# Issuing the whole start of a fused attention and feed-forward kernel from one written list, with eight GpSimd operations on VectorE and added products of zeros on TensorE

## The chip, the core and the metric

The kernel runs on one core of a Trainium2 chip. The metric is the device time of one execution in microseconds. An execution of the kernel before took 555.93 us (median of three, 555.01 to 556.05).

## What is computed

```python
# attention: a, B, C, x per batch (4), head (8), 768 positions; head_dim 32, d_state 16
L = np.exp(cum[:, :, :, None] - cum[:, :, None, :]) * causal      # decay between positions
y_intra = ((C @ B.T) * L) @ x
y_inter = (C @ state) * np.exp(cum)
state = decay_full * state + sum(B x * decay_from_j)              # from chunk to chunk
x = y.transpose(0, 2, 1, 3).reshape(3072, 256)
h = np.maximum(np.maximum(x @ w1, x @ w2), x @ w3)                # first layer, 768 wide
x = h @ w_out
x = (1 / (1 + np.exp(-(x @ w_gate))) * (x @ w_val)) @ w_out2      # second layer, 1536 wide
```

## The kernel before

The positions are cut into 8 chunks of 96, and the 32 pairs of batch and head into 8 groups of four. A step of the attention is one group of one chunk; there are 64 steps. For step k (chunk c, group g) the program makes:

- for k below 16, a masked copy of C on ScalarE (L327); later chunks get B and C split into three bfloat16 parts instead (`split_bc`, with a subtraction on GpSimd, L312, and twelve small transfers into `bi` and `cs`),
- the score products `s` of four units on TensorE (L332 or L335), into one of three PSUM buffers that the hidden layer uses too (tag `up`),
- the decay factors: `load_decay` brings the raw decays of two steps into `dec` (four buffers), broadcast to 128 partitions, and two scans on VectorE (L291) turn them into running products. The decays have to be clipped first: `clip_all` loads all of them, clips them on VectorE and stores them in device memory (`ad`), from where every later load comes; the first two loads are clipped on the spot (L287),
- `mt`: the state part on GpSimd (L340), the weighted scores on VectorE (L347),
- the output products `y` (L356); after four steps the outputs are copied to `xt_hi` (ScalarE, L366) and `xt_lo` (VectorE, L368), and the carried state is transposed into the next chunk's x (`xs`, VectorE, four L372).

The two feed-forward layers work on eight token tiles of 512 columns. For tile t and each of six blocks m of the first layer's width, three banks u are made, each from two times three products of 128x512 (a high and a low half of both operands, L406 to L408); ScalarE copies the first bank (L484), VectorE takes the maximum with the second and third (L486, L488), ScalarE and a low-half operation (GpSimd L479, in the last tiles VectorE) split the result into `hi` and `lo`, and six products add it to the output banks `o` one block later (`down`).

The first layer's weights arrive as 64-bit floats in twelve pieces, a00 to a51 (block, half), and are decoded: three ScalarE operations, one on VectorE (L178), an add on GpSimd (L183), a cast on ScalarE (L211), a low half on GpSimd (L213).

The order of the work is set by generators. Each step, decode or eviction is a generator that stands in `Pipe`; every `tick` moves each one a stage on. Ahead of the tiles 12 steps (`START`) are ticked through, and then one step or more per slot as `UNTIL` says: 24 steps are out when tile 0 ends. `BEHIND` says after which decay load how many weight pieces are loaded. All loads are issued by SyncE's one queue, in program order. The program's scheduler then orders the instructions of each engine.

```python
    for k in range(START + 6):
        if k < START:
            att_step(LEAD)
        if k == 4:
            load_x(1, slice(16, 32))
        pipe.tick()
    for _ in range(9):
        pipe.tick()
        weights_tick()
```

Of the kernel before, what the change touches and what calls it, by code (L numbers as in the profile page):

```python
# [19 lines left out]
CH = 96  # L20
# [21 lines left out]
START = 12  # L42
# [3 lines left out]
LEAD = 2  # L46
# [6 lines left out]
BEHIND = {4: 1, 5: 1, 6: 2, 7: 2, 8: 2, 9: 1, 10: 1, 11: 1, 12: 1}  # L53
# [18 lines left out]
def scan_attention_then_ffn(ctx: ExitStack, tc: tile.TileContext, xh, ah, bch, pick, bn, w1, w2, w3,  # L72
# [56 lines left out]
    def piece1(m, part):  # L129

        cols = slice(256 * m, 256 * m + 256)
        loads = [[up1[0][:, :, cols], up1[1][:, :, cols]],
                 [up1[2][:, :, cols], dn1[:, m, :].rearrange("p (d f) -> p d f", d=2)]][part]
        return wp1, wt1.setdefault(m, []), loads, f"a{m}{part}"

    todo = [(piece1, m, part) for m in range(M1) for part in range(2)]
# [7 lines left out]
    def load_weights():  # L144

        f, m, part = todo.pop(0)
        wpool, blocks, loads, name = f(m, part)
        raw = wpool.tile([128, 2 * len(loads), 128, 2], I32, tag=name, name=f"raw_{name}")
        for k, s in enumerate(loads):
            sp.dma_start(out=raw[:, 2 * k:2 * k + 2].rearrange("p b n t -> p b (n t)"), in_=s)  # L150
        loaded.append((raw, wpool, blocks, name))

    def decode(raw, wpool, blocks, name):
        nb = raw.shape[1]
        second = name[0] != "a"

        def behind(k):
            return tc.issue_after(evict[k].ins) if second else ExitStack()
# [5 lines left out]
        with behind(0):  # L164
            act.activation(out=sg.bitcast(F16).rearrange("p b (n t) -> p b n t", t=2)[..., 1], in_=f1.bitcast(F32),
                           func=AF.Identity, scale=2.0 ** -112)
        if second:
            yield
        with behind(0):
            act.mul(f1.bitcast(F32), f1.bitcast(F32), 2.0 ** -112)  # L170
        if second:
            yield
# [7 lines left out]
        if second:  # L180
            yield
        with behind(1):
            (dve if second else pool).tensor_tensor(out=r, in0=t, in1=r, op=ALU.add)  # L183
        yield
        if second:
            hi, lo = store2(wpool, blocks, name)
            parts = [(r.bitcast(F32), slice(0, 4))]
            if name[0] != "d":
                v = r.bitcast(F32)
                q = wq[0].tile([128, 3, 128], F32, tag="q", name=f"q_{name}")  # L190
                for k, (out, x, y, op) in enumerate(((q[:, 0], v[:, 1], v[:, 3], ALU.add),
                                                     (q[:, 2], v[:, 0], v[:, 1], ALU.subtract),
                                                     (q[:, 1], q[:, 0], v[:, 0], ALU.subtract),
                                                     (v[:, 1], v[:, 2], q[:, 1], ALU.subtract))):
                    with behind(1):
                        dve.tensor_tensor(out=out, in0=x, in1=y, op=op)
                    if k % 2:
                        yield
                parts.append((q, slice(4, 7)))
            for x, at in parts:  # L200
                with behind(0):
                    act.copy(hi[:, at], x)
                yield
            for x, at in parts:
                with behind(1):
                    dve.tensor_tensor(out=lo[:, at], in0=x, in1=hi[:, at].bitcast(F32),
                                      op=ALU.subtract)
            return
        w = wpool.tile([128, 2, nb, 128], F32R, tag=name, name=f"w_{name}")
        blocks += [(w[:, 0, b], w[:, 1, b]) for b in range(nb)]  # L210
        act.copy(w[:, 0], r.bitcast(F32))  # L211
        yield
        pool.tensor_tensor(out=w[:, 1], in0=r.bitcast(F32), in1=w[:, 0].bitcast(F32),  # L213
                           op=ALU.subtract)
# [17 lines left out]
    def constants():  # L232

        pool.memset(delta_s, 0.0)
        for y in ys:
            act.copy(y[:, :, CH + N:128], delta_s[:, 0:4, 0:128 - CH - N])
        for r in range(4):
# [7 lines left out]
            pool.memset(d[:, r, 0:1], 1.0)  # L245
        act.copy(delta, delta_s)
# [7 lines left out]
    pk = acon.tile([128, NG], F32, name="pk")  # L254

    def clip_all():

        t = awk.tile([128, 2, LW], F32, tag="ac", bufs=1, name="ac")
        sp.dma_start(out=t.rearrange("p u w -> p (u w)"),
                     in_=ah.rearrange("r (s w) -> (r s) w", s=4))  # L260
        dve.tensor_scalar(out=t[:, :, 1:LW], in0=t[:, :, 1:LW], scalar1=1e-6, scalar2=1.0,
                          op0=ALU.max, op1=ALU.min)
        yield
        sp.dma_start(out=ad.rearrange("r (s w) -> (r s) w", s=4),
                     in_=t.rearrange("p u w -> p (u w)"))

    def load_decay(n, src):
        t = awk.tile([128, PU, LW], F32, tag="dec", bufs=DECS, name=f"dec{n}")
        i = sp.dma_start(out=t.rearrange("p u w -> p (u w)"), in_=src[n].partition_broadcast(128))
        dec[n] = t  # L270
        for _ in range(BEHIND.get(n, 0)):
            with tc.issue_after(i.ins):
                load_weights()
# [508 lines left out]
```

## Time and profile before

| | us |
|---|---|
| median of three runs | 555.93 |
| the profiled execution, its time | 554.77 |
| the profiled execution, its span | 553.0 |
| TensorE busy in the span | 535.5 |
| VectorE | 384.0 |
| ScalarE | 322.2 |
| GpSimd | 128.2 |
| first product of tile 0 | 36.11 |
| first product of tile 1 | 85.60 |

The span is the time from the first to the last instruction; 1.8 us lie around it. A busy share is an average over stages: the start, in which attention, weights and tile 0 run side by side, is to be read by itself. A row of the timeline gives the start of an instruction (or of a run of the same), how long it is busy, and in brackets how long its engine had waited and for what. TensorE's rows overlap their successors, so that the spacing of two starts is the price of a product, not the length of its row.

### The profile page before, as it was taken

What the parts mean: (1) busy time and instruction counts of PE and PEld (TensorE: products, weight loads), DVE (VectorE), ACT (ScalarE), POOL (GpSimd) and SP (SyncE); (2) the same over time, 40 slices, a digit from 0 to 9 for tenths busy, and PEclk for the clock granted to TensorE, in tenths of its full rate; (3) what the DMA queues carried; (4) which work ended last, traced back from release to release, by engine and by line L of the source; (5) the groups of instructions that cost most, each with busy time, mean ns of one, the idle gap of its engine ahead of it and who ended that gap; (6) DMA issues with size and microseconds to landing.
All of it is one profiled execution on the core that took longest, in us unless ns stands there. A gap on an engine that the chain in (4) does not pass through costs nothing.

```text
span 553.0 us, 7923 instructions
## 1 busy us (share of the span) xinstructions
PE 535.5 (97%) x2885; PEld 429.3 (78%) x2885; DVE 384.0 (69%) x648; ACT 322.2 (58%) x571; POOL 128.2 (23%) x161
## 2 busy tenths in 40 slices
PE   5998999999999999999999999999999999999997
PEld 5777667777677778888888878877888878888885
DVE  4988985676776834799988896586455567554554
ACT  5667745334335223687798886675555565555563
POOL 3568996555555430000000000000000000000000
PEclk9999899999999999999999999999999999999999
DMA  7999985894985118013220000001000002000002
GB/s 234 344 268 241 298 200 87 187 180 142 192 197 125 31 59 321 1 38 118 76 75 0 1 1 2 0 19 58 1 0 2 0 1 77 0 1 0 1 0 76
DMA packets 32150, 50.51 MB, mean 91 GB/s; under 512 B 3184, under 2 KB 18160, under 8 KB 32112
## 3 DMA queue, kind: packets, MB, share of 16 engines
q1 hardware_dynamic: 31824, 49.63, 34.1%
q8 instruction: 22, 0.36, 0.3%
q10 hardware_dynamic: 288, 0.39, 0.2%
q14 instruction: 16, 0.13, 0.1%
HBM read 38.51 MB, written 3.25 MB: 76 GB/s over the span
## 4 chain that ended last, share of the span: by engine, by line
PE 83%; DMA 9%; DVE 4%; ACT 1%; issue 1%; SPq 0%; DVEq 0%; ACTq 0%
PE o L659 17%; PE ug L628 15%; PE uv L628 15%; PE u L406 9%; PE u L408 8%; PE u L407 8%; DMA raw_a<-in_w 6%; PE o L407 3%; PE o L406 3%; PE o L408 3%; DMA dec<-ad 2%; PE y L356 2%; PE s L335 1%; DVE dec L291 1%; DMA ad<-ac 1%
## 5 line engine op out<-in xcount | busy, mean ns | idle before, releaser
L659 PE MATMUL o<-hi,w_d 128*128 128x512 f32 x288 | 97.6, 390 | 0.0
L406 PE MATMUL u<-xt_hi,w_a 128*128 128x512 f32 x216 | 88.4, 409 | 3.7 <-DVE s L488 2.6
L628 PE MATMUL ug<-xt_hi,w_g 128*128 128x512 f32 x252 | 91.5, 392 | 0.1
L628 PE MATMUL uv<-xt_hi,w_v 128*128 128x512 f32 x252 | 90.3, 390 | 0.0
L407 PE MATMUL u<-xt_lo,w_a 128*128 128x512 f32 x216 | 85.8, 397 | 0.1
L408 PE MATMUL u<-xt_hi,w_a 128*128 128x512 f32 x216 | 85.5, 396 | 0.0
L659 PEld LDWEIGHTS o<-hi,w_d 128*128 128x128 f32 x288 | 54.0, 188 | 11.3 <-ACT hi L702 0.2
L703 DVE TENSOR_TENSOR lo<-y,hi 128x512 fp32r<-128x512 f32 x72 | 49.4, 688 | 16.8 <-ACT hi L702 15.9
L291 DVE TENSOR_TENSOR_SCAN dec<-dec,delta 128x388 f32<-128x388 f32 x64 | 57.8, 945 | 1.3 <-DMA dec<-ad 1.1
L477 ACT CAST hi<-s 128x512 fp32r<-128x512 f32 x36 | 22.3, 621 | 61.5 <-DVE s L488 60.9
L659 PE MATMUL o<-lo,w_d 128*128 128x512 f32 x144 | 56.4, 391 | 0.8 <-DVE lo L703 0.8
L628 PEld LDWEIGHTS ug<-xt_hi,w_g 128*128 128x128 f32 x252 | 47.3, 188 | 12.1 <-ACT ug L631 0.9
L628 PEld LDWEIGHTS uv<-xt_hi,w_v 128*128 128x128 f32 x252 | 47.3, 188 | 10.6 <-DVE y L699 0.8
L406 PEld LDWEIGHTS u<-xt_hi,w_a 128*128 128x128 f32 x216 | 41.2, 191 | 13.7 <-POOL mt L340 1.7
L628 PE MATMUL ug<-xt_lo,w_g 128*128 128x512 f32 x126 | 49.1, 390 | 0.0
L628 PE MATMUL uv<-xt_lo,w_v 128*128 128x512 f32 x126 | 49.0, 389 | 0.0
L408 PEld LDWEIGHTS u<-xt_hi,w_a 128*128 128x128 f32 x216 | 41.4, 192 | 9.1
L407 PEld LDWEIGHTS u<-xt_lo,w_a 128*128 128x128 f32 x216 | 41.3, 191 | 8.4 <-DVE xt_lo L368 0.6
L702 ACT CAST hi<-y 128x512 fp32r<-128x512 f32 x72 | 44.4, 620 | 5.8 <-DVE y L699 4.4
L699 DVE TENSOR_TENSOR y<-uv,y 128x512 f32<-128x512 f32 x36 | 24.8, 688 | 30.9 <-PE uv L628 30.7
L486 DVE TENSOR_TENSOR s<-u,s 128x512 f32<-128x512 f32 x36 | 24.8, 688 | 24.6 <-PE u L408 19.4
L636 DVE TENSOR_TENSOR y<-ug,y 128x512 f32<-128x512 f32 x36 | 24.8, 690 | 24.4 <-ACT y L633 17.4
(103 smaller groups left out, 956.9 us busy)
## 6 DMA issues: line engine op xcount, KB each, us to landing
dec<-ad SPq DMA_DIRECT2D x30, 388.0 KB, 5.8
raw_a<-in_w SPq DMA_DIRECT2D x18, 256.0 KB, 6.9
bi<-parts SPq DMA_DIRECT2D x36, 128.0 KB, 5.3
cs<-parts SPq DMA_DIRECT2D x36, 96.0 KB, 5.5
xs<-in_xh SPq DMA_DIRECT2D x6, 512.0 KB, 5.0
raw_g<-in_wg SPq DMA_DIRECT2D x6, 512.0 KB, 5.0
raw_v<-in_wv SPq DMA_DIRECT2D x6, 512.0 KB, 5.9
raw_d<-in_wo SPq DMA_DIRECT2D x6, 512.0 KB, 4.3
```

Of the source, the lines that this page charges most:

```text
L291: dve.tensor_tensor_scan(out=f, data0=f, data1=delta.rearrange("p u w -> p (u w)"), initial=0.0, op0=ALU.mult, op1=ALU.add)
L406: pe.matmul(ps, wlo, a_hi(k), start=k == 0, stop=False)
L407: pe.matmul(ps, whi, a_lo(k), start=False, stop=False)
L408: pe.matmul(ps, whi, a_hi(k), start=False, stop=k == kn - 1)
L477: act.copy(hl[0], s)
L486: dve.tensor_tensor(out=s, in0=banks[1], in1=s, op=ALU.max)
L628: turn[0] = pe.matmul(ps, w, x, start=new and e == 0, stop=e == 2, skip_group_check=not new)
L636: evict[1] = dve.tensor_tensor(out=self.t[k], in0=ps, in1=self.t[k], op=ALU.add)
L659: turn[0] = pe.matmul(acc2[t][d], w, x, start=n == 1 and e == 0, stop=n == M2 and e == 2)
L699: evict[1] = dve.tensor_tensor(out=g, in0=v, in1=g, op=ALU.mult)
L702: act.copy(hl[0], g)
L703: dve.tensor_tensor(out=hl[1], in0=g, in1=hl[0].bitcast(F32), op=ALU.subtract)
```

## The change

Everything up to the end of tile 0 is issued from one text, `ORDER`, whose words are single operations: `Ld3` loads decay 3, `D3a` is one half of its scan, `k5` a masked C, `S5`, `m5`, `bx5`, `y5` the parts of step 5, `H`, `X`, `T` the copies and transposes of an output half, `sg`, `raw`, `r`, `stt`, `add`, `hi`, `lo` with a piece's name its seven decode steps, `F` a hidden bank, `E`, `U`, `V`, `h`, `l` its eviction, `O` the down products, `P` and `Q` the parts and subtractions of a split, `I` an added product. `in_order` walks through the text and makes each instruction follow the one before it on its engine, so that the scheduler has no choice left. Eight of the operations that GpSimd did go to VectorE. The added products multiply zeros (fourteen, `I`) or the scan's constant (one each, `I0` to `I14`) into a bank that nobody reads before it is begun anew. The decays to be clipped come as 64 rows of 4 instead of 128 of 2, x and the states in halves of 16 units, and the loads stand in the text's order. From tile 1 on the program is as before; 24 steps are out, the last block's down products are pending.

```diff
-START = 12
-BEHIND = {4: 1, 5: 1, 6: 2, 7: 2, 8: 2, 9: 1, 10: 1, 11: 1, 12: 1}
+ORDER = """
+LB0 Lx00#0 I a clip Ld0 K delta I0 pk LC0 k3 k1 k4 clip0 Ld1 D0a astore k0 D0b S3 S0 k5 clip1 D1a
...
+IDLE0 = 14
+ON_DVE = """loa10 loa11 adda21 adda30 adda31 adda41 Q30 l3""".split()
...
+        elif kind == "add":
+            (dve if kind + at in ON_DVE else pool).tensor_tensor(out=words[at], in0=highs[at], in1=words[at], op=ALU.add)
...
+            eng, w = dve if kind + at in ON_DVE else pool, wts[at]
+            eng.tensor_tensor(out=w[:, 1], in0=words[at].bitcast(F32), in1=w[:, 0].bitcast(F32),
+                              op=ALU.subtract)
...
+    def idle_product(at):
+
+        if not idle:
+            idle.append(pso.tile([128, TT], F32, tag="o1", name="idle"))
+        z = (delta_s.rearrange("p u w -> p (u w)") if at else sgs[1].rearrange("p b n -> p (b n)")).bitcast(BF16)
+        for _ in range(1 if at else IDLE0):
+            pe.matmul(idle[0], z[:, 0:128], z[:, 0:TT], start=True, stop=True)
...
+    def in_order(text):
+
+        tails, seen, consts = {}, {}, constants()
+        for word in text.split():
+            word, part = (word.split("#") + [None])[0:2]
+            part = seen[word] = seen.get(word, -1) + 1
+            with ExitStack() as order:
+                for i in tails.values():
+                    order.enter_context(tc.issue_after(i))
+                mark = nc.cur_bb.bb.instructions[-1]
+                emit(word, part, consts)
+            new = nc.cur_bb.bb.instructions
+            k = next(k for k in reversed(range(len(new))) if new[k] is mark)
+            for i in new[k + 1:]:
+                tails[i.engine] = i
+
+    in_order(ORDER)
+    done[0] = SHARED
...
-    slot = 0
+    slot = slots
...
-    for t in range(NTT):
+    for t in range(1, NTT):
```

TensorE, from its first instruction. `s0_3` are the scores of chunk 0, group 3, `y0` the output bank of the first four groups, `u` the hidden layer, `sg1` a tile of zeros. Before:

```order
L332 MATMUL s0_0_171<-y1_91 128x96 x4
L332 MATMUL s0_1_177<-y1_91 128x96 x4
L332 MATMUL s0_2_183<-y1_91 128x96 x4
L332 MATMUL s0_3_191<-y1_91 128x96 x4
L356 MATMUL y0_106<-mt0_98,xs0_145 32x112 x4
L332 MATMUL s0_4_208<-y1_91 128x96 x4
L356 MATMUL y0_106<-mt1_99,xs0_145 32x112 x4
L332 MATMUL s0_5_225<-y1_91 128x96 x4
```

Now, from the last of the fourteen products of zeros on:

```order
L670 MATMUL idle_115<-sg1_88 128x512
L670 LDWEIGHTS delta_s_94
L670 MATMUL idle_115<-delta_s_94 128x512
L322 MATMUL s0_3_173<-y1_91 128x96 x4
L322 MATMUL s0_0_178<-y1_91 128x96 x4
L322 MATMUL s0_1_195<-y1_91 128x96 x4
L670 LDWEIGHTS delta_s_94
L670 MATMUL idle_115<-delta_s_94 128x512
L322 MATMUL s0_4_208<-y1_91 128x96 x4
L322 MATMUL s0_2_227<-y1_91 128x96 x4
L670 LDWEIGHTS delta_s_94
L670 MATMUL idle_115<-delta_s_94 128x512
```

The groups stand in another sequence, the outputs further behind the scores, and added products between them; nine more stand together, with three output groups between them, ahead of the last group of chunk 1's first half.

VectorE, from the first decay on (`dec0`, `dec1` the decays of steps 0 to 3, `mt0` the result of step 0). Before:

```order
L287 TENSOR_SCALAR dec0_116<-dec0_116 128x8x96
L291 SCALAR_TENSOR_TENSOR dec0_116<-dec0_116,delta_95 128x388 x2
L287 TENSOR_SCALAR dec1_149<-dec1_149 128x8x96
L347 TENSOR_TENSOR mt0_98<-s0_0_171,dec0_116 128x4x96
L347 TENSOR_TENSOR mt1_99<-s0_1_177,dec0_116 128x4x96
L291 SCALAR_TENSOR_TENSOR dec1_149<-dec1_149,delta_95 128x388 x2
L347 TENSOR_TENSOR mt2_100<-s0_2_183,dec1_149 128x4x96
```

Now:

```order
L618 TENSOR_SCALAR dec0_132<-dec0_132 128x8x96
L273 SCALAR_TENSOR_TENSOR dec0_132<-dec0_132,delta_95 128x388 x2
L618 TENSOR_SCALAR dec1_167<-dec1_167 128x8x96
L273 SCALAR_TENSOR_TENSOR dec1_167<-dec1_167,delta_95 128x388 x2
L345 TENSOR_TENSOR mt3_101<-s0_3_173,dec1_167 128x4x96
L576 SCALAR_TENSOR_TENSOR t_a00_202<-raw_a00_189,sg0_87 128x512
L345 TENSOR_TENSOR mt0_98<-s0_0_178,dec0_132 128x4x96
L273 SCALAR_TENSOR_TENSOR dec2_215<-dec2_215,delta_95 128x388
L345 TENSOR_TENSOR mt1_99<-s0_1_195,dec0_132 128x4x96
```

The scans of both decays now come ahead of the first `mt`, the first decode step stands between the first and the second `mt`, and `mt1` waits behind a scan of `dec2`.

VectorE once more, from the first maximum of the hidden layer on (`s3_0_0` is the running maximum of tile 0, block 0; `w_a10`, `r_a21` belong to weight pieces). Before:

```order
L486 TENSOR_TENSOR s3_0_0_478<-u3_0_0_1_504,s3_0_0_478 128x512
L372 STREAM_TRANSPOSE xs2_324<-y0_106 32x4x32 x4
L347 TENSOR_TENSOR mt5_103<-s1_5_526,dec6_250 128x4x96
L291 SCALAR_TENSOR_TENSOR dec8_332<-dec8_332,delta_95 128x388 x2
L178 SCALAR_TENSOR_TENSOR t_a21_461<-raw_a21_295,sg1_88 128x512
L488 TENSOR_TENSOR s3_0_0_478<-u3_0_0_2_531,s3_0_0_478 128x512
```

Now:

```order
L610 TENSOR_TENSOR s3_0_0_433<-u3_0_0_1_443,s3_0_0_433 128x512
L576 SCALAR_TENSOR_TENSOR t_a11_467<-raw_a11_336,sg1_88 128x512
L585 TENSOR_TENSOR w_a10_465<-r_a10_418,w_a10_465 128x512
L576 SCALAR_TENSOR_TENSOR t_a20_474<-raw_a20_451,sg0_87 128x512
L273 SCALAR_TENSOR_TENSOR dec6_374<-dec6_374,delta_95 128x388
L345 TENSOR_TENSOR mt5_103<-s1_5_459,dec6_374 128x4x96
L610 TENSOR_TENSOR s3_0_0_433<-u3_0_0_2_478,s3_0_0_433 128x512
L576 SCALAR_TENSOR_TENSOR t_a21_492<-raw_a21_456,sg1_88 128x512
L585 TENSOR_TENSOR w_a11_489<-r_a11_421,w_a11_489 128x512
```

Two low halves that were GpSimd's stand here, the four adds follow further down, and the decode steps come earlier by up to three pieces against the maxima.

SyncE's queue begins with B and x instead of the pick matrix and C; the store of the clipped decays stays ahead of the first weight piece, which comes now ahead of the loads of `dec2` to `dec4`.

## Rows read from the trace of the kernel before

**Rows 1.** Busy time by stretch: stretch, length, each engine busy (instructions), granted clock, DMA

```profile
6.65:36.10 29.45, 28.77 (x192) 24.17 (x193) 24.64 (x41) 17.14 (x31) 12.46 (x19) 1.00 1.01 306
43.60:85.60 42.00, 38.15 (x274) 29.06 (x273) 36.21 (x60) 25.49 (x44) 37.12 (x36) 0.96 0.90 225
85.60:122.00 36.40, 36.40 (x277) 27.57 (x276) 24.01 (x39) 17.05 (x29) 23.97 (x28) 1.00 0.88 162
57.00:60.00 3.00, 3.00 (x9) 2.32 (x8) 2.93 (x8) 2.17 (x5) 3.00 (x3) 0.50 0.97 359
```

**Rows 2.** Timeline of TensorE: start, us, engine, line, operation, shapes, count, wait

```profile
13.81 0.60 PE L356 MATMUL y<-mt,xs 128*32 128x112 f32 x8
14.34 2.02 PE L332 MATMUL s<-y 128*128 128x96 f32 x8
16.29 0.60 PE L356 MATMUL y<-mt,xs 128*32 128x112 f32 x8
...
40.98 0.63 PE L408 MATMUL u<-xt_hi,w_a 128*128 128x512 f32 x1
41.40 0.63 PE L407 MATMUL u<-xt_lo,w_a 128*128 128x512 f32 x1
...
43.32 1.03 PE L332 MATMUL s<-y 128*128 128x96 f32 x8
44.13 0.48 PE L406 MATMUL u<-xt_hi,w_a 128*128 128x512 f32 x1
...
54.43 0.51 PE L335 MATMUL s<-cs,bi 96*128 96x96 bf16 x8
56.50 0.58 PE L406 MATMUL u<-xt_hi,w_a 128*128 128x512 f32 x1 [1.56 <-DVE s L488]
...
85.37 0.39 PE L408 MATMUL u<-xt_hi,w_a 128*128 128x512 f32 x1
85.60 0.39 PE L406 MATMUL u<-xt_hi,w_a 128*128 128x512 f32 x1
```

**Rows 3.** Timeline of VectorE

```profile
7.66 0.56 DVE L287 TENSOR_SCALAR dec<-dec 128x768 f32<-128x768 f32 x1 [3.35 <-DMA dec<-in_ah]
...
33.81 0.56 DVE L347 TENSOR_TENSOR mt<-s,dec 128x384 f32<-128x384 f32 x1 [1.90 <-PE s L332]
34.28 0.55 DVE L368 TENSOR_TENSOR xt_lo<-y,xt_hi 128x384 fp32r<-128x384 f32 x1
34.75 1.28 DVE L372 STREAM_TRANSPOSE xs<-y 32x128 f32<-32x128 f32 x4
36.06 0.69 DVE L178 SCALAR_TENSOR_TENSOR t_a<-raw_a,sg 128x512 int32<-128x512 int32 x1
...
43.59 0.69 DVE L486 TENSOR_TENSOR s<-u,s 128x512 f32<-128x512 f32 x1 [1.46 <-PE u L408]
44.20 1.28 DVE L372 STREAM_TRANSPOSE xs<-y 32x128 f32<-32x128 f32 x4
...
77.86 1.80 DVE L291 TENSOR_TENSOR_SCAN dec<-dec,delta 128x388 f32<-128x388 f32 x2
79.58 0.67 DVE L488 TENSOR_TENSOR s<-u,s 128x512 f32<-128x512 f32 x1
```

**Rows 4.** The chain that ended last, in order of time: start, us, what

```profile
4.34 4.54 DMA ad<-ac
8.94 5.77 DMA dec<-ad
```

**Rows 5.** Groups of GpSimd up to 86 us: count, busy us, mean ns, idle before

```profile
L213 POOL TENSOR_TENSOR w_a<-r_a,w_a 128x512 fp32r<-128x512 f32 x12 | 16.9, 1407 | 0.0
L183 POOL TENSOR_TENSOR r_a<-t_a,r_a 128x512 int32<-128x512 int32 x12 | 16.2, 1358 | 3.0 <-DVE t_a L178 3.0
```

**Rows 6.** Groups of VectorE: the decode step up to 86 us, a low half of later weights

```profile
L178 DVE SCALAR_TENSOR_TENSOR t_a<-raw_a,sg 128x512 int32<-128x512 int32 x12 | 13.4, 1119 | 0.1
...
L206 DVE TENSOR_TENSOR w_g<-r_g,w_g 128x512 fp32r<-128x512 f32 x6 | 4.1, 686 | 0.0
```

More of the change, by code (lines that the diff above doesn't have):

```diff
@@ L45 @@
 SHARED = 24
-LEAD = 2
 MTS = 8
@@ L179, in decode @@
                                      op1=ALU.bitwise_or)
-        if second:
-            yield
[L182 to L214, printed above, removed]
+        yield
+        with behind(1):
+            dve.tensor_tensor(out=r, in0=t, in1=r, op=ALU.add)
+        yield
+        hi, lo = store2(wpool, blocks, name)
+        parts = [(r.bitcast(F32), slice(0, 4))]
@@ new lines, in decode @@
+        if name[0] != "d":
+            v = r.bitcast(F32)
+            q = wq[0].tile([128, 3, 128], F32, tag="q", name=f"q_{name}")
+            for k, (out, x, y, op) in enumerate(((q[:, 0], v[:, 1], v[:, 3], ALU.add),
+                                                 (q[:, 2], v[:, 0], v[:, 1], ALU.subtract),
+                                                 (q[:, 1], q[:, 0], v[:, 0], ALU.subtract),
+                                                 (v[:, 1], v[:, 2], q[:, 1], ALU.subtract))):
+                with behind(1):
+                    dve.tensor_tensor(out=out, in0=x, in1=y, op=op)
+                if k % 2:
+                    yield
+            parts.append((q, slice(4, 7)))
@@ L216, in weights_tick @@
+        for x, at in parts:
+            with behind(0):
+                act.copy(hi[:, at], x)
+            yield
+        for x, at in parts:
+            with behind(1):
+                dve.tensor_tensor(out=lo[:, at], in0=x, in1=hi[:, at].bitcast(F32),
+                                  op=ALU.subtract)
     def weights_tick(last=True):
@@ L267, in load_decay @@
[L267 to L273, printed above, removed]
-    def load_x(c, part=slice(0, NU)):
-        if c not in xs:
-            xs[c] = awk.tile([128, NU, D], F32, tag="xs", name=f"xs{c}")
-            bx[c] = awk.tile([128, NU, N], F32, tag="bx", name=f"bx{c}")
-        for t, src, n in ((xs[c], xh, D), (bx[c], bn, N)):
-            sp.dma_start(out=t[:, part].rearrange("i u d -> i (u d)"),
-                         in_=src[:, c, n * part.start:n * part.stop])
@@ L348, in attention, with outputs @@
                                         op=ALU.mult)
+    def outputs(k):
+        c, g = steps[k]
+        lead = None
+        for i in [g] if k < SHARED else (g, g - 3, g - 2, g - 1) if g % 4 == 3 else []:
+            for q in range(4):
+                with tc.issue_after(lead.ins) if lead else ExitStack():
+                    i_y = pe.matmul(ys[g // 4][32 * q:32 * q + 32, i % 4, 0:CH + N],
+                                    xs[c, g // 4][:, 4 * (i % 4) + q, :],
+                                    mt[(k + i - g) % MTS][:, q, :], start=True, stop=True)
+            lead = lead or i_y
@@ new lines, in halves, with high, low, attention @@
+    def halves(c, h):
+        o = (c * CP + 2 * CH * h) % RING
+        return [ys[h][:, :, 0:CH].rearrange("p (b k) i -> p b k i", k=KD)] + [
+            v[:, :, o:o + 2 * CH].rearrange("p k (b i) -> p b k i", b=2) for v in (xt_hi, xt_lo)]
+    def high(c, h):
+        src, hi, lo = halves(c, h)
+        act.copy(hi, src)
+    def low(c, h):
+        src, hi, lo = halves(c, h)
+        dve.tensor_tensor(out=lo, in0=src, in1=hi.bitcast(F32), op=ALU.subtract)
+    def attention(k, ahead):
+        c, g = steps[k]
+        score(k)
+        for _ in range(ahead + 1):
+            yield
+        states(k)
+        weigh(k)
```

334 lines of the change are left out of this document (213 added, 121 removed).

## The prediction

> **What bounds the kernel now.** I read the span in stretches first (busy time by stretch), because the change ends where token tile 0 ends. In [rows 1] TensorE is busy 28.77 of 29.45 us from its first score product to the first product of the hidden layer, 38.15 of 42.00 us up to the first product of tile 1, and 36.40 of 36.40 after that. From 85.60 us on the only thing worth having is fewer products, and the change removes none there. So all that it can win lies before 85.60 us, and the question is when tile 1 starts.
>
> Then the timeline of TensorE. A step of the attention is one score group `s` and one output group `y`; [rows 2] show them at a steady period: 0.53 us from `y` to `s`, 1.95 us from `s` to the next `y`, 2.48 us together, with no wait between. One `s` group later, at 43.32 us, the same work is over 0.81 us after its start. The hidden-layer products show the same two speeds: 0.42 us from start to start at 40.98, 0.23 us at 85.37. So TensorE ran at 1.2 GHz until about 43 us; the granted clock of 1.00 that [rows 1] give for 6.65 to 36.10 us can't be right, and the spacing of the rows decides. TensorE was the bound of that stretch: twelve steps at 2.48 us are 29.8 us. What it did before the rise was 3 us of 128x512 products without a pause; 29 us of small products without a pause had not brought it. The stretch 57 to 60 us has a granted clock of 0.50 [rows 1], and what went before that fall was small products and a wait of 1.56 us for VectorE [rows 2].
>
> Third, VectorE's timeline and groups. From 43.60 to 85.60 us it is busy 36.21 of 42.00 us and GpSimd 37.12 of 42.00 [rows 1]: in that stretch these two and TensorE are all near full, and each waits for another.
>
> The profiled execution took 554.77 us, 1.2 below the median of 555.93. I make the sum as a difference and apply it to the median.
>
> **The change part by part.** (a) *Until the first hidden-layer maximum.* It stands at 43.59 us [rows 3] and ends the first two banks of the hidden layer. In the change the products of zeros keep TensorE busy from its first microseconds: fourteen at 0.42 us (the price of a 128x512 product at 1.2 GHz, [rows 2]) are 5.9 us, and the first `s` can't start before its masked C, whose load now stands behind `dec0`; `dec0` had landed at 7.66 [rows 3], so the C lands at about 8 and the first `s` starts about 8.5 instead of 6.65, with nothing lost by the fourteen. I take it that TensorE is then at 2.4 GHz for most of the attention. With `s` at 0.81 it is no bound, and the list of VectorE is. Its clock there: `dec0` clipped at 7.7, two scans, `dec1` clipped (about 10: 0.6 MB behind `dec0` at the 306 GB/s of [rows 1] is 2 us), two scans and a first `mt` are done at about 12.5. The next scan needs `dec2`, which goes through device memory: the store of the clipped `a` takes 4.54 us and the load of `dec2` 5.77 [rows 4], and it came at 14.7. The clipped `a` now stands behind two 256 KB loads, so I take 15.0. The decode step of a00 and `mt0` stand ahead of that scan and fit into the wait.
>
> From the scan of `dec2` on, the rows of VectorE's list up to the last `xt_lo` of tile 0's columns, at the spacing from one start to the next in [rows 3] (scan 1.72 for two, 0.86 each; `mt` 0.47; `xt_lo` 0.47; transposes 1.31 for four; decode step 0.69): 8 scans 6.9, 10 `mt` 4.7, 3 `xt_lo` 1.4, transposes 1.3, decode step 0.9 with a little waiting: 15.2 us, so 30.2. The first product needs this `xt` and the low half of a00, which GpSimd makes in the same microseconds. Twelve products at 0.23 bring the maximum to 33.1, and I add 0.9 for handoffs: 34.0 against 43.59, **-9.6**. If the clock is not held, this term is another; that is the first rival.
>
> (b) *From there to the first product of tile 1:* 42.0 us before (43.59 to 85.60). Here VectorE gets eight operations from GpSimd: four adds, two low halves, one `lo`, one split of B and C. One such costs GpSimd 1.36 to 1.41 us in [rows 5] and VectorE 0.69 (a low half, [rows 6]), 0.60 from start to start. VectorE's rows from the first maximum to the decode step of the last weight piece a51: 10 maxima at 0.60 (6.0), 9 scans (7.7), 8 `mt` (3.8), two sets of transposes (2.6), one `xt_lo` (0.5), 9 decode steps, 7 moved operations at 0.60 and the split at 1.05 (896 columns to 512). The decode step takes 0.69 where GpSimd is idle (36.06, [rows 3]) and 1.12 on average beside it [rows 6]: 0.43 of waiting. I take 0.35 of it, since GpSimd loses eight operations, for the nine decode steps (8.6) and for the eight moved ones (5.25 + 2.8). The sum is 37.2. Behind it a51 needs an add and a low half on GpSimd, 1.36 + 1.41 [rows 5], a cast on ScalarE between (0.6, about a VectorE maximum's spacing), and six products (1.4); then six of the down projection (1.4): 6.2. Together 43.4, **+1.4**. TensorE's own work in this stretch, 96 hidden-layer and 30 down products at 0.23 and the small ones, is about 36 us and stays below.
>
> The row of the decode step shows that VectorE waits beside GpSimd [rows 6]. The Trainium skill (SBUF — State Buffer, "SBUF: two separate sides") gives the rule: a VectorE operation with two SBUF inputs and a GpSimd operation hold one pair of ports in turn, each for its whole length, the other blocked. This trace agrees for the decode step, 0.69 against 1.12; by the rule all eight moved operations wait too, which is the 2.8 above, and without it the sum would be 2.8 lower.
>
> (c) *Four products of the down projection* that before came after 85.60 are now done ahead of it: 4 x 0.23, **-0.9**.
>
> (d) *Work left for tile 1.* Four scans (3.4) and two sets of transposes (2.6) that were done before 85.60 now stand behind tile 0's last maximum: 6.0 us. VectorE has 12.4 us free in tile 1 [rows 1], but the score groups wait for it: between 0 and 6, I take **+1.5**.
>
> (e) *Handoffs in one fixed list.* The list has no second choice where a load comes late. One place shows: `dec4` reuses `dec0`'s buffer, so SyncE's queue stands still until `mt1` is out (about 16.4), and the B of chunk 1, the second half of chunk 0's x and all later loads queue behind it; they come about 20 to 23 and are wanted at about 21. Bounds 0 and 3 us, taken **+1.0**. The weight loads get earlier: two decay loads and 0.9 MB of x and B that stood ahead of the last weight piece now stand behind it; with VectorE as the bound I cost that at nothing. The added products cost nothing while TensorE waits, and 0.42 each where it doesn't: at most 15 x 0.42 = 6 us, which is in the rivals.
>
> Sum: -9.6 + 1.4 - 0.9 + 1.5 + 1.0 = -6.6, **549.3 us**, for this case 546.5 to 552.
>
> **Rivals.** *1. The clock falls again before tile 0 and TensorE stays the bound (slower).* Between 12.9 and 16.4 us TensorE has, by (a), one `s` group and one or two added products, and small products with a wait went before the one fall of the trace [rows 2]. From 16.4 everything is then at 1.2 GHz: six `s` groups 11.7, four `y` 2.1 and two added products 0.9 bring it to about 31; the nine added products and three `y` that follow take 5.4, to 36.5. *1a:* those nine, nearly 128x512 products alone, bring the clock back, as the first ones of the hidden layer did before: two more `s`, five `y` and twelve products at full speed give the maximum at 41.9: -1.7 in place of -9.6, so 557.2. *1b:* they don't, and the rise comes within the hidden layer as now: two `s` and five `y` at half speed (6.6) and twelve products at 0.42 (5.1) give the maximum at 48, +4.6, so 563.5, less what late products find ready, 561 to 563. For: 29 us of `s` and `y` did not raise the clock. Against: fourteen large products precede, and if the wait for `dec2` is shorter, TensorE has hardly a pause. It decides whether the row of `s` shows 0.8 or 1.9 us at 17 to 30 us.
>
> *2. Better than the sum:* the moved operations meet no GpSimd work (-2.8) and tile 1 swallows its extra work (-1.5): 545.0. For: GpSimd's own load falls. Against: its remaining operations are the longest ones.
>
> *3. The change of order does nothing for the time,* because the loads set tile 0's end: then about 556. Against: the last piece is now queued ahead of 1.7 MB that it stood behind, 5 us at 306 GB/s [rows 1].
>
> **How the numbers follow.** Forecast 0.44, rival 2 0.13, 1a 0.24, 1b 0.14, rival 3 0.05. The range leaves out the far ends of rival 2 and 1b: 545.5 to 560.5. A measurement can tell about 0.2%, 1.1 us. Faster by more: the forecast and rival 2, and a small part of 1a: 0.60. Same: most of rival 3 and a third of 1a: 0.12. Slower: 0.28.
>
> **What would show it.** Right: `s` groups of 0.8 us after 17 us; first maximum at 33 to 36; tile 1's first product 76 to 79; VectorE busy over 0.9 between them. Wrong: `s` of 1.9 us and no wait of TensorE between 17 and 36; a decode step waiting over 2 us for a load; TensorE waiting for VectorE in tile 1 by more than 3 us.

## The result and the profile after

The changed kernel took 560.61 us (median of 15 runs, 557.12 to 562.51), the kernel before 555.93 in the runs beside it: a ratio of 1.0088 with a 95% interval of 1.0069 to 1.0106, so 0.9% slower. The ratio leaves out one run of the kernel before, of 1048.49 us; its other fourteen lie between 553.61 and 556.76. The profiled execution is the longest of the 15: 562.51 us with a span of 560.7. Its span is 7.7 us longer than that of the profiled execution before, while the medians are 4.7 apart, so the differences below are those of two executions and add up to more than the change of the median.

The span falls apart at the first products of the tiles. A tile has 108 hidden products, so that the 109th is the first of tile 1 and the 217th the first of tile 2.

| us | before | after | difference |
|---|---|---|---|
| first maximum of the hidden layer | 43.59 | 37.86 | -5.7 |
| from there to the first product of tile 1 | 42.01 | 43.97 | +2.0 |
| first product of tile 1 | 85.60 | 81.83 | -3.8 |
| from there to the first product of tile 2 | 40.19 | 51.45 | +11.3 |
| from there to the end of the span | 427.2 | 427.4 | +0.2 |

So the start gained 3.8 us, and tile 1, in which the program is the old one, lost 11.3. That loss is not one of this execution alone: in three runs below that leave the loads of tile 1 as they are (e1, e2, h2) tile 1 takes 50.3 to 50.8 us. Busy time by stretch, of before (tile 1 alone, since [rows 1] end earlier):

```profile
85.60:125.79 40.19, 40.19 (x294) 30.68 (x293) 27.11 (x46) 17.45 (x30) 23.98 (x28) 1.00 0.90 168
```

and of after: from the first score to the first maximum, to tile 1, tile 1, and two stretches within tile 1:

```profile
8.92:37.86 28.94, 25.79 (x225) 19.95 (x225) 23.52 (x38) 20.95 (x37) 13.34 (x19) 0.88 0.91 302
37.86:81.83 43.97, 39.60 (x279) 29.22 (x280) 42.02 (x66) 30.32 (x50) 28.41 (x30) 1.00 0.85 174
81.83:133.28 51.45, 44.35 (x289) 32.78 (x288) 32.53 (x58) 17.59 (x30) 25.24 (x32) 0.90 0.92 214
...
94.20:97.60 3.40, 3.40 (x10) 2.65 (x9) 3.28 (x5) 0.86 (x2) 2.54 (x6) 0.50 0.33 121
111.30:118.10 6.80, 5.09 (x16) 3.47 (x17) 1.53 (x4) 2.21 (x4) 2.84 (x2) 0.50 0.59 199
```

In tile 1 of before TensorE is busy for all of its 40.19 us. After, it is busy 44.35 of 51.45: 7.1 us are waits, and the other 4.2 are about the price of the lower clock, half of the 3.40 + 5.09 us that TensorE worked in the two stretches at 0.50. That accounts for the 11.3 to about 0.9 us: four products of the down projection, 0.23 us each, are no longer in tile 1, so about as much of TensorE's work there stays unexplained.

The timeline of TensorE shows the start (answering to [rows 2]) and the waits of tile 1:

```profile
10.44 2.02 PE L322 MATMUL s<-y 128*128 128x96 f32 x16 [0.39 <-ACT y L311]
...
22.60 5.41 PE L322 MATMUL s<-y 128*128 128x96 f32 x24 [1.03 <-DMA y<-in_bch]
...
84.11 0.33 PE L325 MATMUL s<-cs,bi 96*128 96x96 bf16 x4 [0.75 <-DMA cs<-parts]
93.06 0.50 PE L428 MATMUL u<-xt_hi,w_a 128*128 128x512 f32 x1 [2.21 <-DVE s L510]
113.01 0.48 PE L325 MATMUL s<-cs,bi 96*128 96x96 bf16 x4 [4.14 <-DMA dec<-ad]
```

A score group is four products and stands as eight rows (x8) in the trace. At 10.44 two groups take what one took before; the three at 22.60, behind a wait for chunk 1's B, are slow again: the granted clock is 1.00 to 22.5, 0.51 to 29.4 and then 1.00. In tile 1 the clock falls at 94.2, behind the wait that ended at 93.06, and at 111.3, within the one that ended at 113.01.

Where these waits come from stands in SyncE's queue. Before:

```profile
76.40 0.58 SPq L297 DMA_DIRECT2D bc<-in_bch  x1
77.97 0.33 SPq L269 DMA_DIRECT2D dec<-ad  x1
79.74 0.33 SPq L280 DMA_DIRECT2D xs<-in_xh  x1
88.61 1.85 SPq L308 DMA_DIRECT2D bi<-parts  x3
...
97.14 0.55 SPq L308 DMA_DIRECT2D cs<-parts  x1
```

After:

```profile
79.25 0.52 SPq L257 DMA_DIRECT2D dec<-ad  x1
...
87.54 0.33 SPq L290 DMA_DIRECT2D bc<-in_bch  x1
89.02 0.33 SPq L257 DMA_DIRECT2D dec<-ad  x1
92.83 0.33 SPq L264 DMA_DIRECT2D bx<-in_bn  x1
95.24 0.33 SPq L257 DMA_DIRECT2D dec<-ad  x1
97.31 0.33 SPq L264 DMA_DIRECT2D bx<-in_bn  x1
97.72 2.17 SPq L298 DMA_DIRECT2D bi<-parts  x3
...
106.91 0.55 SPq L298 DMA_DIRECT2D cs<-parts  x1
```

Chunk 4's B and C (`bc`) were loaded 9 us ahead of tile 1, now 6 us behind its start; the last of the twelve transfers that its split needs was issued at 97.14, now at 106.91. The score at 113.01 is put down to a decay's landing, but a score reads only `bi` and `cs`: the last of the twelve landed 5.9 us behind its issue, at 112.8. Decay 12, the first row of after, is issued at 79.25 (before at 57.35), and VectorE's scans wait for it; the maximum that TensorE waits for at 93.06 stands behind these scans and a set of transposes on VectorE:

```profile
84.90 1.81 DVE L273 TENSOR_TENSOR_SCAN dec<-dec,delta 128x388 f32<-128x388 f32 x2 [2.86 <-DMA dec<-ad]
```

### The profile page after: what moved, and what is told of

Read it like the earlier page. It is cut to its first block, busy times and chain, and to the rows that moved or that the text cites. A ratio compares the mean times of both kernels' runs of the same rounds, so it can differ in the third digit from the quotient of the medians.

```text
span 560.7 us, 7987 instructions
## 1 busy us (share of the span) xinstructions
PE 536.0 (96%) x2914; PEld 423.2 (75%) x2914; DVE 389.1 (69%) x656; ACT 323.6 (58%) x571; POOL 114.9 (20%) x153
## 4 chain that ended last, share of the span: by engine, by line
PE 77%; DVE 9%; DMA 7%; ACT 2%; issue 2%; SPq 1%; POOL 1%; DVEq 0%; POOLq 0%; ACTq 0%
PE o L812 17%; PE uv L781 15%; PE ug L781 15%; PE u L428 7%; PE u L430 6%; PE u L429 6%; DMA dec<-ad 3%; DVE dec L273 3%; PE o L428 2%; PE o L429 2%; PE o L430 2%; PE y L355 2%; DMA cs<-parts 1%; PE s L322 1%; PE s L325 1%
## 5 line engine op out<-in xcount | busy, mean ns | idle before, releaser
L812 PEld LDWEIGHTS o<-hi,w_d 128*128 128x128 f32 x288 | 54.0, 188 | 11.3 <-ACT hi L855 0.2
L499 ACT CAST hi<-s 128x512 fp32r<-128x512 f32 x30 | 18.6, 620 | 52.1 <-DVE s L510 51.6
L855 ACT CAST hi<-y 128x512 fp32r<-128x512 f32 x72 | 44.4, 619 | 5.7 <-DVE y L852 4.3
L786 ACT COPY sv<-uv 128x512 f32<-128x512 f32 x36 | 21.2, 588 | 33.5 <-PE uv L781 33.4
```

What stands on the lines that cost most here:

```text
L499: act.copy(hl[0], s)
L786: evict[0] = act.copy(self.temp(1 if i == 6 else 2), ps)
L812: turn[0] = pe.matmul(acc2[t][d], w, x, start=n == 1 and e == 0, stop=n == M2 and e == 2)
L855: act.copy(hl[0], g)
```

## The experiments

**Theory A** was that tile 1's loads stand too late in SyncE's queue. **Theory B**, the rival, that VectorE's work is what is late: the eight moved operations, and the scans left for tile 1. All ratios are against the kernel before on the same chip; the columns after them are of the one profiled execution of each run.

The first maximum moves from execution to execution. Eight of these profiles have the same list up to there (the changed kernel, e2, e3, e4, f1, f2, f3 and g1), and it came at 35.93 to 38.94 us. A difference of up to 3 us in that column is therefore not by itself the effect of an edit; the lengths of tile 1 differ by far more.

| run | median | ratio [95%] | first maximum | tile 1 starts | its length |
|---|---|---|---|---|---|
| e1_no_idle | 561.55 | 1.0112 [1.0085, 1.0138] | 37.31 | 81.27 | 50.78 |
| e2_pool8 | 563.73 | 1.0156 [1.0129, 1.0182] | 38.35 | 84.91 | 50.72 |
| e3_xafter | 561.01 | 1.0104 [1.0082, 1.0126] | 36.77 | 80.78 | 49.03 |
| e4_loads | 558.82 | 1.0067 [1.0043, 1.0091] | 38.65 | 82.61 | 48.34 |
| f1_b4x | 555.32 | 1.0006 [0.9990, 1.0022] | 35.93 | 79.89 | 46.08 |
| f2_loads2 | 556.15 | 1.0021 [0.9994, 1.0048] | 37.11 | 81.09 | 45.14 |
| f3_both | 554.28 | 0.9976 [0.9955, 0.9997] | 38.09 | 82.06 | 43.80 |
| f5_lb1 | 555.41 | 0.9998 [0.9980, 1.0016] | 37.54 | 81.50 | 45.39 |
| g1_chunk3 | 552.98 | 0.9966 [0.9945, 0.9987] | 38.94 | 84.94 | 40.28 |
| g2_noidle | 556.00 | 1.0007 [0.9987, 1.0027] | 37.92 | 81.86 | 44.01 |
| g3_before14 | 557.23 | 1.0040 [1.0026, 1.0054] | 48.85 | 89.84 | 39.28 |
| h2_m1 | 559.25 | 1.0087 [1.0060, 1.0114] | 35.59 | 79.53 | 50.30 |
| h1_best | 551.97 | 0.9943 [0.9927, 0.9958] | 38.84 | 82.80 | 40.28 |
| h3_fill | 553.08 | 0.9950 [0.9930, 0.9970] | 35.65 | 82.24 | 41.34 |
| h4_a50 | 551.69 | 0.9935 [0.9913, 0.9956] | 35.98 | 81.07 | 41.95 |

### Without the added products

```diff
-LB0 Lx00#0 I a clip Ld0 K delta I0 pk ...
+LB0 Lx00#0 a clip Ld0 K delta pk ...
```

> The changed kernel without any added product. Theory A (the time is lost in tile 1, whose loads come late in SyncE's queue; the products of zeros are what shortened the start): TensorE is at 1.2 GHz from its first score group on, thirteen groups at 1.95 us and ten output groups at 0.53 from 8.9 us bring the hidden layer to about 39.5 and its first maximum to about 44 instead of 37.9; tile 1 starts 2 to 6 us later than 81.8: 562 to 567 us. Rival (the products of zeros gain nothing, or cost): 560 us or less, first maximum still near 38.

It was the rival by its first maximum, 37.31, within the spread of the eight; the time, 561.55, lies between the two forecasts. The interval overlaps the changed kernel's. The timeline of TensorE, and the stretches on both sides of the place where the spacing of the products changes:

```profile
9.06 9.48 PE L322 MATMUL s<-y 128*128 128x96 f32 x56 [9.06 <-ACT y L311]
18.47 0.78 PE L355 MATMUL y<-mt,xs 128*32 128x112 f32 x24
```

```profile
9.00:14.87 5.87, 5.81 (x27) 5.81 (x28) 5.23 (x8) 4.44 (x9) 1.73 (x4) 1.00 0.70 220
14.87:18.50 3.63, 3.63 (x35) 3.38 (x35) 3.45 (x6) 2.38 (x5) 0.70 (x2) 1.00 0.89 325
```

27 rows of score products in 5.87 us, then 35 in 3.63: 0.22 and 0.10 us each. The clock rose after 5.8 us of score groups alone, seven of which stand in a row. The granted clock of 1.00 in the first of the two rows is as wrong as it was in [rows 1]. In the changed kernel it is the zeros that raise it, within their row: their spacing falls from 0.43 to 0.22 us at 5.5 us, and the first score group is already fast.

```profile
1.78 4.99 PE L670 MATMUL idle<-sg 128*128 128x512 bf16 x14 [1.78 <-POOL sg L156]
8.92 1.13 PE L322 MATMUL s<-y 128*128 128x96 f32 x8 [1.92 <-ACT y L311]
```

So the zeros do bring the clock up, but they are not needed for it, and the first maximum is not earlier for them. That the new order is what lets the scores alone do it is not shown: the kernel before began with four score groups in a row, 7.2 us without a pause, and stayed at half clock.

### The eight operations back on GpSimd

```diff
-ON_DVE = """loa10 loa11 adda21 adda30 adda31 adda41 Q30 l3""".split()
+ON_DVE = []
```

> The changed kernel with the eight moved operations back on GpSimd. Theory B (VectorE's load sets tile 0's end and what is left for tile 1): VectorE was busy 42.0 of 44.0 us between the first maximum and tile 1, and the eight took 8.5 us of it; GpSimd has room (28.4 of 44.0). Tile 1 starts 3 to 8 us earlier and the time falls to 552 to 557. Theory A (the late loads of tile 1): tile 1 starts earlier, but its products wait for the same loads, so most is given back: 558 to 562.

Neither: 3 us slower than the changed kernel, and tile 1 starts 3.1 us later although VectorE has less to do in tile 0. The waits of TensorE from the first maximum to tile 1:

```profile
PE o L429 <- POOL lo L614: 1.9, 1, 1.9
PE u L428 <- POOL w_a L585: 1.8, 1, 1.8
```

Each weight piece needs an add and a low half one after the other; with all of them GpSimd is busy 39.3 of the 46.6 us of this stretch (28.4 of 44.0 in the changed kernel), and TensorE waits for it twice. The clock also fell for 3.4 us there, at 44.4, which may be part of the later start of tile 1. The move was worth its price, and theory B's first half falls.

### Loads one at a time

e3 puts chunk 5's x behind chunk 4's twelve transfers:

```diff
             for dst, src in routes(c, parts, p):
-                sp.dma_start(out=dst, in_=src)
+                moved[0] = sp.dma_start(out=dst, in_=src)
...
+            with tc.issue_after(moved[0].ins) if moved[0] else ExitStack():
                 sp.dma_start(out=t.rearrange("i u d -> i (u d)"), in_=src[:, c, n * h:n * h + n])
```

> The changed kernel, with chunk 5's x and states loaded behind chunk 4's twelve transfers of split B and C instead of ahead of them. Theory A: the last of the twelve is issued some 5 to 9 us earlier than 106.9, TensorE's wait of 4.1 us at 108.9 to 113.0 and the fall of its clock behind it go: 553 to 557 us. Theory B (VectorE's scans left for tile 1 are what is late): the wait is only renamed, 559 to 562.

No change, which is theory B's number. But the twelve were issued only 2 to 3 us earlier, because they start with chunk 4's B and C, which were still loaded at 86.6. TensorE still waits 3.7 us. I had moved the second thing in the queue, not the first.

e4 loads what tile 1 needs as soon as a buffer is free:

```diff
-... Pd32 V5 Ld12 D12a Lx30#0 Lx30 h5 l5 O4 D12b Ld13 Lx40#0 Lx31#0 Lx31 Ld14 Ld15 ...
+... Lx30#0 Lx30 Lx31#0 Lx31 Ld12 Pd30#0 ... Ld13 Pd30#1 ... Ld15 Ld14 Pd30#3 ...
```

> The changed kernel, with the decays 12 to 15 and chunk 3's x and states loaded as soon as their buffers are free, ahead of or between chunk 3's twelve transfers instead of behind them. Theory A: the scans' waits of 2.9 and 0.2 us at 82 to 87 go, and with them TensorE's wait of 2.2 us at 93 and the clock's fall at 94.2; the later wait of 4.1 us shrinks: 553 to 558 us. Theory B (the work of the scans, not their loads): 559 to 562, with VectorE's wait gone and TensorE's wait still there. Misgiving: the twelve transfers come later and delay tile 0's last scores, +1 to +2.

Faster by 1.8 us in the medians, with intervals that overlap, between the two forecasts, and the misgiving came true. Timeline of TensorE in tile 1:

```profile
90.31 0.48 PE L325 MATMUL s<-cs,bi 96*128 96x96 bf16 x4 [5.72 <-DMA xs<-in_xh]
112.62 0.33 PE L325 MATMUL s<-cs,bi 96*128 96x96 bf16 x4 [1.02 <-DMA dec<-ad]
```

The wait of 2.2 us at 93 is gone and that of 4.1 us is 1.0, but a score of chunk 3 now waits 5.7: decays 12 to 15 wait for their buffers in SyncE's queue, and chunk 3's transfers wait behind them.

### The head of the queue, and both

f1 adds the word `Lb4` (chunk 4's B and C) to the list, ahead of the first `Pd32`, to e3's edit. f2 places e4's loads where the queue need not wait long: chunk 3's x ahead of `Pd30#0`, `Ld12` ahead of `Pd31#0`, `Ld13` ahead of `Pd30#3`, and `D12a` ahead of `H21`. f3 is both.

> The changed kernel, with chunk 4's B and C loaded as soon as chunk 3's are read (78 us) instead of at 87.5, and chunk 5's x and states behind chunk 4's twelve transfers. Theory A, second form (chunk 4's split starts too late in SyncE's queue: its last transfer was issued at 106.9 and TensorE waited for it until 113.0; before it was issued at 97.1): the twelve are out by about 98, the wait of 3.7 to 4.1 us and the clock's fall behind it go, the wait of 2.2 us at 93 stays: 555 to 557 us. Theory B (VectorE's leftover scans): no change, 560 to 561.

> The changed kernel, with chunk 3's x and states and the decays 12 and 13 loaded ahead of and between chunk 3's transfers, at points where SyncE's queue needn't wait long, and the first scan of decay 12 ahead of the last copies of the outputs. Theory A: VectorE's wait of 2.9 us at 82 goes and with it the 2.2 us of TensorE at 93, without the 5.7 us at 90 that the first attempt put there; the wait at 113 stays: 557 to 559 us. Theory B: TensorE's wait at 93 stays, 560 to 561.

> Both edits together. Theory A: tile 1 without waits over 1 us and without a fall of the clock, 41 us long as before instead of 51: 550 to 553 us, faster than both kernels. Theory B: 558 or more. If only one of the two waits is real, the other comes up in its place: 555 to 557.

f1, which moves nothing but loads, came out at theory A's number and f2 better than that. f3 fell short of it: slightly faster than the kernel before (0.9976), but its tile 1 was 43.8 us long, not 41. SyncE's queue of f1 shows the head where it belongs, and TensorE's waits over 0.5 us in its tile 1 what is left:

```profile
76.05 0.33 SPq L554 DMA_DIRECT2D bc<-in_bch  x1
```

```profile
84.30 0.33 PE L327 MATMUL s<-cs,bi 96*128 96x96 bf16 x4 [2.89 <-DMA bi<-parts]
93.18 0.51 PE L430 MATMUL u<-xt_hi,w_a 128*128 128x512 f32 x1 [0.69 <-DVE s L512]
113.55 0.50 PE L430 MATMUL u<-xt_hi,w_a 128*128 128x512 f32 x1 [0.92 <-DVE s L512]
```

The waits did not go as forecast one by one: the one at 93, which was to stay, shrank to 0.7 us, and a score of chunk 3 waited 2.9 us at 84.3 for its split instead of 0.8.

f5 is f3 with `LB1` ahead of `Ld4` and the load of a01 behind them.

> Both edits, and at the start chunk 1's B ahead of decay 4 and the second decoded weight piece behind it. VectorE waited 1.8 us for decay 4 at 21.9 and TensorE 1.0 us for this B at 22.6, where its clock fell. If these loads set the first hidden maximum: at 35 to 36 instead of 37.9, and 1 to 2 us less than with both edits alone. If VectorE's own work sets it: the same to 0.5 us.

The first maximum came at 37.5 and the time was no better than f3's. Decay 4 still landed at 22.1 (21.8 in the changed kernel): its load waits for `mt1`, and this order of the loads did not change that.

### Chunk 3's split earlier

g1 puts all of chunk 2's transfers (`Pd20` to `Pd22`) ahead of `Ld10`, `Lb3` behind it, `P30`, `Q30`, `P31`, `Q31`, `P32` each a few operations earlier, and chunk 3's transfers, its x, decays 12 and 13 and chunk 4's B and C behind `Lx21`.

> The version with both edits at the seam, and chunk 3's split a step earlier too: chunk 2's remaining transfers go into SyncE's wait of 7.7 us ahead of decay 10, chunk 3's B and C are loaded behind them, its casts and subtractions stand earlier on their engines. What was left of the loss in that version is one wait of 2.8 us of TensorE at 86.4 for a score of chunk 3, with the clock's fall at 87.8. Theory A (SyncE's queue at the seam): both go, tile 1 is 41 us long instead of 43.8: 551 to 552.5. If VectorE's leftover work is under it: the wait is renamed, 554.

Tile 1 is as long as before the change, 40.28 us with 0.6 of waits, and the whole is 0.3% faster than the kernel before. Its busy time by stretch:

```profile
84.94:125.22 40.28, 39.69 (x290) 30.03 (x289) 31.39 (x57) 17.49 (x30) 24.76 (x31) 1.00 0.95 199
```

What was lost at the seam is back: 51.45 to 40.28 us, although VectorE still does 31.4 us of work in tile 1 (27.1 before the change). So theory B's second half falls too. It began later, though, at 84.94: the subtraction `Q30`, moved ahead, stands ahead of a maximum on VectorE, and TensorE waited 1.8 us at 69.5, where the clock fell; with it back in its place (h1) that wait was 0.8 us and the clock held.

### The products of zeros by themselves

g2 is f3 without any added product, g3 the kernel before with the first fourteen:

```diff
+    for _ in range(14):
+        pe.matmul(zeros, z[:, 0:128], z[:, 0:TT], start=True, stop=True)
     sp.dma_start(out=pk, in_=pick)
```

> The version with both edits at the seam, without any added product. After the first look without them (the clock rose at 14.9 us by the scores alone): the same time to 1 us, 553.5 to 555.5. If the products of zeros are worth what they were put in for: 556 or more.

> The kernel before, with only the fourteen products of zeros ahead of its first score. If products of this shape bring the clock up before the attention and it holds: twelve steps at 1.34 instead of 2.48 us less the waits for loads, the first hidden maximum 4 to 9 us earlier than 43.6: 547 to 552. If the alternation of scores and outputs lets it fall again: 554 to 556, the same as before.

g2 falls at the edge of the second forecast, 1.7 us above f3, with intervals that overlap: the products of zeros are worth a small gain at most, and none is shown. g3 is slower than before by 0.4%. Its TensorE:

```profile
7.49 2.81 PE L332 MATMUL s<-y 128*128 128x96 f32 x24
13.03 1.10 PE L332 MATMUL s<-y 128*128 128x96 f32 x8 [2.73 <-DVE mt L347]
14.06 0.60 PE L356 MATMUL y<-mt,xs 128*32 128x112 f32 x8
15.20 1.99 PE L332 MATMUL s<-y 128*128 128x96 f32 x8 [0.54 <-ACT y L327]
17.12 0.60 PE L356 MATMUL y<-mt,xs 128*32 128x112 f32 x8
...
40.72 0.80 PE L406 MATMUL u<-xt_hi,w_a 128*128 128x512 f32 x1 [4.47 <-POOL w_a L213]
```

The zeros did bring the clock up: three groups in 2.81 us. Then TensorE had to wait 2.7 us for VectorE, the clock fell at 14.05, and the alternation of scores and outputs ran at half speed to the hidden layer, as in [rows 2]. Why the low half of a00 came late at 40.7 was not tried.

### What sets the start

h2 moves one word in the changed kernel, h1 puts everything together (g1 with h2's word moved, `Q30` and `P31` back in their places, `Q31` with them, and `Ld12` ahead of `Pd31`), h3 fills a wait of h1, h4 moves one load of h3.

```diff
-... m0 Ld2 D2a Ld3 m1 ...
+... m0 m1 Ld2 D2a Ld3 ...
```

> The changed kernel with one word moved: mt1 ahead of the first scan of decay 2 instead of behind it, so that the load of decay 4 does not wait for decay 2's arrival. If that order sets the first maximum: decay 4 is issued at about 15 us instead of 16.2 to 19, lands by 20 to 21.5, the first maximum comes at 35 to 36.5, and the time falls by 1 to 2.5 us (558 to 559.5). If the clock's fall sets it: decay 4 lands earlier, but the first maximum stays at 37 to 38 and the time within 1 us of 560.6.

> Everything together: both edits at the seam, chunk 2's transfers in SyncE's wait ahead of decay 10, chunk 3's B and C loaded behind them with its subtractions where they were, and mt1 ahead of decay 2's scan. If each gives what it gave alone: tile 1 starts at 80 to 82 us, is 40.5 us long, 549.5 to 551.5, faster than the kernel before by 0.6 to 1.0%. If the loads of the start are bound by what the memory moves and not by their order: as g1, 552 to 553.5.

In h2 the first maximum came at 35.59, 2.3 us earlier than in the profile of the changed kernel; f1, without the moved word, has 35.93. To tell the order's part, take the time from the landing of decay 2, which itself moved between 14.7 and 17.5 us, to the first maximum, in the profiles whose clock did not fall between 17 and 36 us: 20.9, 20.6 and 20.6 us with the old order (f1, e3, f3), 19.2, 19.4 and 19.4 with `mt1` ahead (h2 and, from below, h3 and h4). The word is worth about 1.4 us there. A fall of the clock in that time can cost more: the five profiles with the old order and such a fall took 20.8 to 23.1 us, the changed kernel's the longest, and h1, with `mt1` ahead, took 22.4: its clock fell at 19.9 us, behind a wait of 1.5, and came back at 30.2. In h2's tile 1 TensorE waited 8.5 us instead of 7.1, and the ratio stayed that of the changed kernel, 1.0087. h1 is 0.6% faster than the kernel before, between its two forecasts.

```diff
-... I2 S5 S7 D2b ...
+... I2 S5 I15 I16 I17 I18 I19 I20 S7 D2b ...
```

> The best version so far with six more added products in TensorE's wait at 16.7 to 18.2 us, ahead of the last score group of chunk 0. If the fall of the clock behind that wait is what the start loses: the granted clock holds to beyond 30 us, the first maximum comes at 35 to 36.5 instead of 38.8, and the median is 1 to 3 us lower: 549 to 551. If the fall has to do with what comes after (the small output products): first maximum at 38 to 39, 551.5 to 553.

The clock held and the first maximum came at 35.65 as foretold. The time did not follow. One reason is that the fall in h1's profile was not typical of it: that profile has the lowest mean granted clock of h1's twelve runs, 0.989; six of them have 1.000, so no fall at all, and their median of 551.9 us is that of the others (552.1). There was little to fill, and that the six products held the clock is not shown, since h2 held it without them. ScalarE's timeline shows another:

```profile
62.43 0.80 ACT L160 ACTIVATE sg<-raw_a 128x512 f16<-128x512 f32 x1 [4.37 <-DMA raw_a<-in_w]
```

g1's order had put the second half of a50 behind chunk 2's transfers; with the earlier start that became a wait.

> The version with the filled wait, with the second half of weight piece a50 loaded ahead of chunk 2's twelve transfers instead of behind them. If that load was what gave the early start back: it lands by about 52 us, tile 0 is 47.2 us long again, tile 1 starts at 79 to 80 us, 548.5 to 550.5. If the weights' loads cap tile 0 whatever their order: another wait of ScalarE or VectorE in its place, 551 to 553.

Tile 1 started at 81.07, 1.7 us earlier than in h1, and was 41.95 us long instead of 40.28; the medians (551.69 and 551.97) are the same. In these profiles most of what the start still gains is gone again by the end of tile 1; that the next late load takes it is argued, not shown, and whether another order of the loads keeps it was not tried.

## Why the prediction was wrong

It said 549.3 us, with 545.5 to 560.5 as its range and 0.6 on faster; the time was 560.61, slower. By its own terms, in the profiled executions:

- **(a) Until the first maximum, -9.6:** -5.7, and -4.7 to -7.7 in the eight profiles of this list. TensorE did run at 2.4 GHz for most of the attention, and VectorE's list came in its place, as written. The zeros did raise the clock, but without them it is up in time as well (e1). The size was off because VectorE's list does not run through. It starts at 14.76, as forecast at 15.0, but waits for decay 4 (1.8 us at 21.9) and for scores (1.2 us at 26.3, within the stretch at half clock, and 1.0 at 32.6), together about the 3.9 us that were missing:

```profile
14.76 0.96 DVE L273 TENSOR_TENSOR_SCAN dec<-dec,delta 128x388 f32<-128x388 f32 x1 [0.55 <-DMA dec<-ad]
...
21.90 0.96 DVE L273 TENSOR_TENSOR_SCAN dec<-dec,delta 128x388 f32<-128x388 f32 x1 [1.78 <-DMA dec<-ad]
...
26.34 0.56 DVE L345 TENSOR_TENSOR mt<-s,dec 128x384 f32<-128x384 f32 x1 [1.15 <-PE s L322]
```

 With `mt1` ahead of the scan and the clock held, the first maximum comes at 35.6 (h2, h3).
- **(b) To tile 1, +1.4:** +2.0. The mechanism held: VectorE is busy 42.02 of 43.97 us. It ends the decode step of a51 37.2 us behind the first maximum, as the sum of its rows had it; what stands behind that took 6.8 us instead of 6.2:

```profile
74.35 0.66 DVE L576 SCALAR_TENSOR_TENSOR t_a<-raw_a,sg 128x512 int32<-128x512 int32 x1
```

 Its waiting beside GpSimd came in another form than the 0.35 us on each operation: few long ones. Groups of VectorE up to 86 us, and one decode step with GpSimd's add beside it:

```profile
L576 DVE SCALAR_TENSOR_TENSOR t_a<-raw_a,sg 128x512 int32<-128x512 int32 x12 | 10.2, 854 | 0.2 <-ACT raw_a L570 0.2
...
L585 DVE TENSOR_TENSOR w_a<-r_a,w_a 128x512 fp32r<-128x512 f32 x2 | 2.5, 1229 | 0.0
```

```profile
39.30 1.62 POOL L579 TENSOR_TENSOR r_a<-t_a,r_a 128x512 int32<-128x512 int32 x1 [1.46 <-DVE t_a L576]
39.67 1.79 DVE L576 SCALAR_TENSOR_TENSOR t_a<-raw_a,sg 128x512 int32<-128x512 int32 x1
```

 The decode step takes 0.85 us on average instead of 1.12 [rows 6], ten of the twelve 0.66 to 0.69. The one at 39.67 us took 1.79: it started 0.37 us after an add of GpSimd that lasted 1.62, and ended 0.5 us behind it. The Trainium skill (SBUF — State Buffer, "SBUF: two separate sides") says that a VectorE operation with two SBUF inputs and a GpSimd operation that reads SBUF share a pair of ports, which the first of them holds for its whole instruction while the other is blocked; this row agrees.
- **(c) Four products less behind the start of tile 1, -0.9:** the count came true, 36 products of the down projection in tile 1 instead of 40, but (d) buries it.
- **(e) Handoffs, +1.0:** in (a) above. The place that it named, decay 4 behind `mt1`, was the right one.
- **(d) Work left for tile 1, +1.5:** tile 1 took 11.3 us longer, with (c) in it, beyond the 6 that I had as the upper bound of (d). This is the step that failed. It counted VectorE's work for tile 1 and not the loads that this work and the scores need. The sentence that let it through stands under (e): what is moved behind the last weight piece in SyncE's queue, "with VectorE as the bound I cost that at nothing". It was not two decay loads and 0.9 MB, but all of tile 1's: decays 12 to 15, chunk 3's and 4's x, chunk 4's B and C, and behind these the twelve transfers of its split. The bound of tile 0 is VectorE, but these loads are for a tile in which TensorE is the bound, and it paid 7.1 us of waiting and 4.2 at half clock. The runs f1, f3 and g1 show it: f1, which moves loads alone, takes 5.3 us off the median, and with loads and the casts, subtractions and one scan that go with them moved, tile 1 is back at 40.28 us.

Of the rivals, the first saw the clock's fall and its return among the nine added products, but had the fall ahead of 16.4 us and the first maximum at 41.9; they came at 22.5 and 37.9. The third named the loads, but at tile 0's end. None had the loads of the tile behind. The sign that I had named for being wrong, TensorE waiting for VectorE in tile 1 by over 3 us, named the place: TensorE waited 7.1 us there, but only 2.2 of them for VectorE and 4.9 for transfers.

## What to carry to other kernels

Where a list ends and an old program takes over, price the seam: for each queue, what stood ahead of it before and what stands behind it now, up to the first consumer in the next stage, and not only the stage that was rewritten. Here a load was in time or not by its place in the in-order queue that issues it: look for the first load that waits for a buffer, and at everything behind it. When one edit removes a wait and the time stays, look for the same wait with a new name before giving up the theory; here it took three moves of loads to get tile 1 back. And before a difference between two profiles is called the effect of an edit, look at the same stretch in other executions of the same program: the first maximum moved by 3 us without any edit, and one profile of h1 showed a fall of the clock that half of its runs did not have.

## What the runs showed of the hardware

Score products of 128x96 without a pause raised the clock after 5.8 us (e1), while in the kernel before four such groups (7.2 us) and then 22 us of alternating scores and outputs did not; what decides between them is open. Waits of 1.0 to 2.7 us stood within 1.2 us of a fall of the clock in the changed kernel (22.5, 94.2) and in g3 (14.05); yet h2 held it through a wait of 1.87 us at 18.2, and h1 lost it behind one of 1.53 us at the same place. So in these runs a wait of this length was a risk and not a rule. The place of the falls changed from one execution to the next: of the eight with one list up to the first maximum, five had a fall between 17 and 36 us and three had none.

The landing of decay 2, which goes through device memory, moved between 14.7 and 17.5 us in these eight; in the three without such a fall the first maximum came 20.6 to 20.9 us behind it.
